# Chunk-selected attention followed by a hard-swish MLP on one core: second batch's keys and queries loaded in two parts, weights asked for earlier, results of batches 1 to 3 turned by DMA

## The chip, the cores and the metric

The kernel runs on 1 core of one Trainium2 chip. The metric is the device time of an execution in microseconds (us), lower is better. The kernel before takes 296.59 us (median of 3 runs, 296.14 to 297.43).

A core has a matrix engine (PE, with its weight loads shown apart as PEld), a vector engine (DVE), a scalar engine (ACT), a general engine (POOL) and a queue engine (SP) that here only issues DMAs. DMAs can be issued from SP, ACT and POOL; each engine works through its own list of instructions in order.

## The reference

Attention of 4 batches, 8 heads, 768 tokens, head size 64. For each query an upper bound of its score with each chunk of 32 keys is made from the chunk's minima and maxima. The 6 chunks with the largest bounds are kept, everything else is masked, and softmax and the product with the values follow. The result, 3072 tokens of 512 channels, goes through an MLP of 512 to 2048 to 512 with a hard-swish between.

```python
k_min = np.min(k_chunks, axis=3); k_max = np.max(k_chunks, axis=3)
ub = np.sum(np.maximum(q[:, :, :, None, :] * k_min[:, :, None, :, :],
                       q[:, :, :, None, :] * k_max[:, :, None, :, :]), axis=-1)
ub = np.where(causal, ub, -1000000000.0)
top_chunks = np.argsort(ub, axis=-1)[..., -top_k:]
...
scores = np.where(mask, scores, -1000000000.0)
scores = scores - np.max(scores, axis=-1, keepdims=True)
attn = np.exp(scores)
attn = attn / (np.sum(attn, axis=-1, keepdims=True) + 1e-09)
...
x = np.ascontiguousarray(attn_out.transpose(0, 2, 1, 3)).reshape(B * S, H * D)
...
h = x @ w_in
relu6 = np.clip(h + 3.0, 0.0, 6.0)
g = h * relu6 / 6.0
return (g @ w_out).astype(np.float32)
```

All inputs and the output are float32.

## The kernel before

The heads are taken two at a time (a pair, 16 pairs, 4 to a batch), the tokens of a batch in two halves of 384. A unit is two pairs of one half, so a batch has four units: units 0 to 3 are batch 0, units 4 to 7 batch 1, and so on. Batch b, half h of the MLP needs the attention results of all four pairs of that half.

For a unit the steps are these. Keys and queries come into SBUF. In batch 0 they come as token blocks (`load_quad`, the DMAs of L144) and PE turns them (L298). From batch 1 on they come as 32-by-32 squares with 128 bytes to a row (`load` and `squares`, the DMAs of L152) and DVE turns them (L308, tiles KF and QF). DVE reduces the keys of each chunk to maximum and minimum (L320, L321, tile KMA) and POOL subtracts. ACT makes relu of the queries (L330, QR). PE makes the bounds (L351, UBT), for all four pairs of a half together from batch 1 on, ACT or DVE copies them out (UBS), PE turns them back (L361, UBN), DVE finds the sixth largest and the selection (L370 to L388, SELA), PE turns that (L394, MP) and ACT and DVE copy it as mask rows into the queries (L179, L181, QLA). PE multiplies keys and queries (L414, SPS), ACT takes the exponential (L424, PT), POOL cuts the diagonal blocks to triangles (L429), PE multiplies with the values (L442, PVP) and DVE divides into the result tile Xb (L450, L451).

For the MLP, `turn_tokens` lets PE turn the 384 tokens by 512 channels of Xb in twelve 128-by-128 transposes (L462, XTP), and `turn_tokens_out` lets DVE copy them from PSUM to SBUF in two copies (L466, tile XT). `hidden` makes 16 groups of four matmuls (L471, HP), ACT makes U from each (L476) and DVE makes GT from U and HP (L481). `result` makes three token blocks of sixteen matmuls (L488, OP), ACT or DVE scales them into OT (L494, L496), and SP stores OT (L500). There are two OT buffers, so the third OT waits until the first is stored. HP, OP, XTP, UBT, UBN, MP and PVP share four PSUM banks.

The order on every engine is made beforehand. `Plan` holds each step with an engine, an assumed length, a rank, what it follows and what buffers it takes and gives. `order` runs through them in assumed time, gives each free engine the ready step of least rank, and the instructions are then written in that order. Nothing is reordered on the chip, so a step that is late holds back all that stands behind it on its engine. A load is a step on SP and an arrival (`arrive`). `load_inputs` puts in the loads of keys and queries of a unit, `load_unit_values` those of the values, and `attend` calls both for the unit three further on, if that unit is of a first half. A load that follows in a buffer waits until the buffer's last reader is done. The DMAs issued from SP and ACT signal through eight semaphores used in turn, so a DMA also waits for the one eight before it.

The weights w_in and w_out come by four DMAs issued from POOL (`load_win`, `load_wout`, L236 and L240), 1024 KB each in SBUF. They are held back: a copy of one element of the values, `seen` (L234), makes them wait until a chosen load of batch 0's values has landed.

Of the kernel before, what the change touches and what calls it, by code (L numbers as in the profile page):

```python
# [13 lines left out]
FP32 = mybir.dt.float32  # L14
# [85 lines left out]
def kernel(  # L100
# [42 lines left out]
            part = (slice(None), slice(None), i) if by_head else (slice(None), i)  # L143
            engine.dma_start(to[part], x[part])  # L144

    def squares(engine, to, x, st):


        for j in range(2):
            for e in range(2):  # L150
                r = 64 * j + 32 * e
                engine.dma_start(to[r:r + 32, :, :],  # L152
                                 x[st["b"], st["h"] + j].rearrange("(c p) d -> p c d", p=CH)[:, :, 32 * e:32 * e + 32])

    def load_quad(n, name, x, engine, by_head=None):

# [3 lines left out]
            st[name, "in", half] = to  # L160
        blocks(engine, to, x, n, by_head)

    def load(st, name, x):

        st[name] = src_pool.tile([P, NCH, 32], FP32, name=name, tag=name.lower())
        squares(nc.sync, st[name], x, st)

    def load_quad_values(n):
        blocks(nc.sync, VS[:, n % 2, units[n][1] * HB:units[n][1] * HB + HB, :, :], v, n, None)
# [60 lines left out]
    def load_win(part):  # L230

        if part == 0:
            seen = const.tile([1, 1], FP32, name="seen")
            nc.gpsimd.tensor_copy(seen[:], VS[0:1, 1, NBLK - 1, 3, 0:1])  # L234
        c0, c1 = part * DFF // 2, (part + 1) * DFF // 2
        nc.gpsimd.dma_start(WIN[:, :, c0:c1], moe_w_in[:, c0:c1].rearrange("(a p) n -> p a n", p=P))  # L236

# [217 lines left out]

    def turn_tokens(g, a):
        if a == 0:
            g["XT"] = GT_pool.tile([P, KT_HID, HS], BF16, name="XT", tag="xt")
        XTP = g["XTP", a] = bank("XTP", [P, 2, HS], BF16)
        for kt in range(a, a + 2):  # L460
            for t in range(HB):
                nc.tensor.transpose(XTP[:, kt - a, t * P:(t + 1) * P],  # L462
                                    X_tiles[g["b"], g["half"]][:, t, kt * P:(kt + 1) * P], IDENTB[:])

    def turn_tokens_out(g, a):
        nc.vector.tensor_copy(g["XT"][:, a:a + 2, :], g["XTP", a][:])  # L466

    def hidden(g, f):
        HP = g["HP", f] = bank("HP", [P, HS])
        for kt in range(KT_HID):  # L470
            nc.tensor.matmul(HP[:], lhsT=WIN[:, kt, f * P:(f + 1) * P], rhs=g["XT"][:, kt, :],  # L471
                             start=(kt == 0), stop=(kt == KT_HID - 1))

    def hidden_relu(g, f):
# [32 lines left out]
    def later(f, *args):  # L507
        return lambda *engine: f(*args, *engine)
# [10 lines left out]
    def load_inputs(n, after=()):  # L519
        two, half = units[n]  # L520
        for name, x in (("KS", k), ("QS", q)):
            if n == 0:
                plan.room[name.lower()] -= 1
                for st in two:
                    there[name, st["pair"], 0] = add("DMA", 0.75, 0)
            elif n < 4:
                arrive((name, two[0]["pair"], half), "SP", 1.6, 1.8, later(load_quad, n, name, x, nc.sync), take=[name.lower()])
                there[name, two[1]["pair"], half] = there[name, two[0]["pair"], half]
        if n >= 4:
            for st in two:  # L530
                for name, x in (("KS", k), ("QS", q)):
                    arrive((name, st["pair"], 0), "SP", 2.2, 2.5, later(load, st, name, x), after=after, take=[name.lower()])
                    there[name, st["pair"], 1] = there[name, st["pair"], 0]

    def load_unit_values(n, after=()):
        two, half = units[n]
# [14 lines left out]
    load_unit_values(3)  # L551
    for name, f, length in (("WIN", load_win, 5.6), ("WOUT", load_wout, 6.2)):
        for part in range(2):
            arrive((name, part), "POOL", 0.9, length, later(f, part), after=[there["V", 2, 1]])


    vs = ["gt", 2 * H // 2]
# [68 lines left out]
    def attend(u):  # L626
# [15 lines left out]
        for i, st in enumerate(two):  # L642
            p = st["pair"]
            need = [mask[i, 0], mask[i, 1]] + made["EB", p % 6] + made["Q", p, half] + made["K", p, half]
            if half == 1:
                need += made["K", p, 0]
            parts = []
            tiles = len(PLAN[half])
            for t in range(tiles):
                cols = max(c0 + w for _, _, w, c0 in PLAN[half][t])  # L650
                a = add("PE", 2 * cols / 2370 + 0.02, r + 8.0 * (i * tiles + t) / (2 * tiles), later(scores, st, half, t),
                        after=need + ([order_of_scores] if order_of_scores else []), take=["s"])
                order_of_scores = a
                begun.append(a)
                free.setdefault(("KL", p), []).append(a)
                free.setdefault(("QL", st["q", half]), []).append(a)
                e = add("ACT", 0.08 + 2 * cols * 0.845e-3, r, later(exponentials, st, half, t), after=[a], take=["pt"],
                        give=[["s", 1]])
                parts.append(e)
                for jb, q0, w, c0 in PLAN[half][t]:  # L660
                    if q0 == jb * P:
                        parts.append(add("POOL", 0.4, r - 15, later(triangle, st, half, t, c0), after=[e]))
            if st["b"] == 0:
                parts.append(add("ACT", 0.45, r - 3, later(cast_values, st, half), after=[there["V", p, half]], give=[vs]))
                parts.append(made["ones", p])
                if half == 1:
                    parts.append(made["V", p])
                else:
                    made["V", p] = parts[-2]
            else:  # L670
                if half == 0:
                    made["V", p] = add("POOL", 0.9, r - 6, later(cast_values, st, half),
                                       after=[there["V", p], made["ones", p % 6]] + free.get(("VB", p - 6), []), give=[["vt", 1]])
                parts.append(made["V", p])
            key = st["b"], half
            a = add("PE", 0.4 if half == 0 else 0.95, r + 1, later(values, st, half), after=parts + finished.get(key, [])[-1:],
                    take=["m"] if finished.get(key) else ["m", "x"],
                    give=[["pt", 1] for _ in range(tiles)])
            if i == 1:
                if 4 <= n + 3 < len(units) and units[n + 3][1] == 0:  # L680
                    load_inputs(n + 3, begun[:1])
                    load_unit_values(n + 3, begun[:1])
            free.setdefault(("VB", p), []).append(a)
            finished.setdefault(key, []).append(
                add("DVE", 0.72, r + 1, later(values_out, st, half), after=[a] + finished.get(key, []),
                    give=[["m", 1]]))
# [9 lines left out]
    for (b, half), xs in finished.items():  # L696
        g = dict(b=b, half=half)
        x = ["x", 2]
        xt, before = [], []
        for a in range(0, KT_HID, 2):  # L700
            m = add("PE", 0.35, r, later(turn_tokens, g, a), after=xs + before, take=["m"] + (["xt"] if a == 0 else []), give=[x])
            before = [m]
            xt.append(add("DVE", 0.5, r - 2000, later(turn_tokens_out, g, a), after=[m], give=[["m", 1]]))
# [47 lines left out]
```

## Time and profile before

| | |
|---|---|
| Time, median of 3 runs | 296.59 us (296.14 to 297.43) |
| Time of the profiled execution | 297.46 us |
| Span of the profiled execution, first to last instruction | 295.7 us |
| PE busy with HP (L471), 512 matmuls | 91.1 us |
| PE busy with OP (L488), 384 matmuls | 90.1 us |
| PE busy with SPS (L414), 320 matmuls | 51.1 us |
| ACT busy with PT (L424), 96 | 85.4 us |
| ACT busy with U (L476), 128 | 71.7 us |
| DVE busy with GT (L481), 128 | 66.8 us |
| PE transposes of Xb (L462), 96 | 38.8 to 249.9 us, first and last start |
| Bytes moved by DMA | 29.81 MB |

The page of the profile gives, for the one core, the busy time of each engine, the span in 40 slices of 7.4 us with the busy share of each slice in tenths, the chain of waits that ended last, followed back from the last instruction, and the costliest groups of instructions by line. The trace behind it can be asked for one line or tile, for the order of instructions of one engine in a window, for the busy time of each engine in a window, and for DMA traffic by queue in a window. Times in it are microseconds from the start of the span. In a row of the chain or of a timeline the first number is the start, the second the time it took, and a mark such as x4 says how many instructions are merged into the row. Engine names with a q (SPq, ACTq) are the engine's issuing of DMAs and its waits, which are not counted as busy time.

### The profile page before, as it was taken

Reading aid. Unit: us, or ns where it says so; the run is one execution under the profiler, and the core shown is the slowest. Engines: PE = TensorE matmul, PEld = TensorE weight load, DVE = VectorE, ACT = ScalarE, POOL = GpSimd, SP = SyncE. Lnnn points to the kernel's source line nnn. Section 1 sums busy time; section 2 is a strip of 40 time slices with the busy share of each in tenths; the row PEclk is TensorE's granted clock in tenths of the full one; section 3 lists DMA queues with packets and bytes.
Section 4 is the critical chain, followed back from the end, with each engine's and each line's share of the span. In section 5 each row is a group of like instructions: output and inputs, shape, how many; then the busy total and the mean of one; then the engine's idle time right before and its main releaser. Section 6 shows DMA issues by size and latency. Waiting matters only on the chain.

```text
span 295.7 us, 6670 instructions
## 1 busy us (share of the span) xinstructions
PE 270.6 (92%) x2384; PEld 161.3 (55%) x2384; DVE 210.7 (71%) x643; ACT 203.1 (69%) x334; POOL 131.5 (44%) x296
## 2 busy tenths in 40 slices
PE   2788799998799999999899989999999999999994
PEld 1445466644444666654565545556566656545641
DVE  6989656793789889998798988987468513831820
ACT  2769889920865899963769986687469863843821
POOL 7778935465370758775722798721111111000000
PEclk9979799999999999999999999999999999999999
DMA  8999999999304299961289991100110001002011
GB/s 169 217 220 137 192 199 217 187 134 198 96 2 87 66 173 173 137 119 73 62 137 183 133 198 41 39 0 2 42 67 0 2 37 73 1 22 88 0 38 71
DMA packets 119746, 29.81 MB, mean 101 GB/s; under 512 B 113568, under 2 KB 115616, under 8 KB 119712
## 3 DMA queue, kind: packets, MB, share of 16 engines
q1 hardware_dynamic: 114976, 24.78, 46.9%
q0 software_dynamic: 3136, 4.19, 8.3%
q10 hardware_dynamic: 1600, 0.39, 0.7%
q8 instruction: 19, 0.31, 0.5%
q14 instruction: 15, 0.12, 0.2%
HBM read 27.26 MB, written 6.29 MB: 113 GB/s over the span
## 4 chain that ended last, share of the span: by engine, by line
PE 57%; DVE 14%; SPq 10%; ACT 7%; DMA 5%; issue 4%; POOL 2%; DVEq 0%; ACTq 0%; POOLq 0%
PE OP L488 21%; PE HP L471 19%; SPq L152 8%; PE SPS L414 7%; PE PVP L442 4%; PE UBT L351 4%; ACT PT L424 2%; DVE GT L481 2%; DMA out_dram<-OT 2%; DVE KMA L320 2%; DVE KMA L321 2%; DVE QLA L181 1%; DMA KS<-in_k_dram 1%; SPq L174 1%; ACT QLA L179 1%
## 5 line engine op out<-in xcount | busy, mean ns | idle before, releaser
L471 PE MATMUL HP<-XT,WIN 128*128 128x384 bf16 x512 | 91.1, 326 | 4.2 <-DVE GT L481 2.0
L424 ACT ACTIVATE PT<-SPS 128x1024 bf16<-128x1024 f32 (+1 forms) x96 | 85.4, 921 | 9.3 <-PE SPS L414 8.3
L488 PE MATMUL OP<-WOUT,GT 128*128 128x512 bf16 x384 | 90.1, 379 | 0.1
L481 DVE SCALAR_TENSOR_TENSOR GT<-U,HP 128x384 bf16<-128x384 bf16 x128 | 66.8, 549 | 23.8 <-ACT U L476 20.4
L476 ACT ACTIVATE U<-HP,THREE 128x384 bf16<-128x384 f32 x128 | 71.7, 589 | 10.6 <-PE HP L471 6.2
L429 POOL TENSOR_SCALAR_AFFINE_SELECT PT<-PT 128x256 bf16<-128x256 bf16 x96 | 38.2, 413 | 75.4 <-ACT PT L424 73.8
L471 PEld LDWEIGHTS <-WIN 128*128 128x128 bf16 x512 | 48.9, 98 | 36.6 <-issue 6.8
L488 PEld LDWEIGHTS <-GT 128*128 128x128 bf16 x384 | 36.6, 98 | 38.1 <-issue 1.2
L414 PE MATMUL SPS<-QLA,KL 128*128 128x384 bf16 (+2 forms) x320 | 51.1, 281 | 2.0 <-ACT PT L424 1.1
L253 POOL TENSOR_SCALAR_AFFINE_SELECT QLA<-QF 64x384 bf16<-64x384 f32 x64 | 33.3, 520 | 20.1 <-PE SPS L414 11.0
L494 ACT ACTIVATE OT<-OP 128x512 f32<-128x512 f32 x22 | 13.1, 596 | 38.7 <-PE OP L488 31.4
L414 PEld LDWEIGHTS <-KL 128*128 128x128 bf16 x320 | 29.0, 98 | 19.5 <-issue 3.9
L253 POOL TENSOR_SCALAR_AFFINE_SELECT KL<-KF 64x384 bf16<-64x384 f32 x64 | 32.5, 509 | 5.9 <-DVE KF L308 2.8
L442 PEld LDWEIGHTS <-PT 128*128 128x128 bf16 x672 | 24.8, 98 | 7.3 <-issue 1.6
L442 PE MATMUL PVP<-VB,PT 128*128 128x65 bf16 x672 | 26.6, 194 | 1.2 <-POOL PT L429 0.6
L330 ACT ACTIVATE QR<-QF 128x384 f32<-128x384 f32 x32 | 16.7, 526 | 11.2 <-DVE QF L308 10.5
L450 DVE RECIPROCAL RINV<-PVP 128x6 f32<-128x6 f32 x32 | 6.0, 186 | 20.9 <-PE PVP L442 20.8
L181 DVE COPY QLA<-MP 32x384 bf16<-32x384 bf16 x42 | 14.8, 353 | 7.5 <-ACT QLA L179 6.0
L320 DVE TENSOR_REDUCE KMA<-KF 128x12 f32<-128x384 f32 x32 | 17.1, 536 | 3.7 <-PE UBT L351 2.3
L451 DVE TENSOR_TENSOR Xb<-PVP,RINV 128x384 bf16<-128x384 f32 x32 | 17.8, 558 | 1.1
L377 DVE MAX8 T<-UB 128x8 f32<-128x24 f32 x192 | 17.7, 167 | 0.0
L321 DVE TENSOR_REDUCE KMA<-KF 128x12 f32<-128x384 f32 x32 | 17.2, 539 | 0.0
(55 smaller groups left out, 203.6 us busy)
## 6 DMA issues: line engine op xcount, KB each, us to landing
out_dram<-OT SPq DMA_DIRECT2D x24, 256.0 KB, 2.0
KS<-in_k_dram SPq DMA_DIRECT2D x52, 96.0 KB, 3.8
QS<-in_q_dram SPq DMA_DIRECT2D x48, 96.0 KB, 3.7
VT<-in_v_dram SPq DMA_DIRECT2D x24, 192.0 KB, 4.1
WIN<-in_moe_w_in_dram POOLq DMA_DIRECT2D x2, 1024.0 KB, 12.0
WOUT<-in_moe_w_out_dram POOLq DMA_DIRECT2D x2, 1024.0 KB, 22.0
VS<-in_v_dram SPq DMA_DIRECT2D x12, 128.0 KB, 3.8
KS<-in_k_dram SPq DMA_DIRECT2D x9, 128.0 KB, 3.8
```

What stands on the lines that cost most here:

```text
L152: engine.dma_start(to[r:r + 32, :, :], x[st["b"], st["h"] + j].rearrange("(c p) d -> p c d", p=CH)[:, :, 32 * e:32 * e + 32])
L253: nc.gpsimd.affine_select(out=to, in_=x, pattern=[[0, n]], compare_op=A.is_ge, fill=0.0, base=0, channel_multiplier=0)
L320: nc.vector.tensor_reduce(out=over, in_=chunks, axis=X_AXIS, op=A.max)
L321: nc.vector.tensor_reduce(out=low, in_=chunks, axis=X_AXIS, op=A.min)
L414: nc.tensor.matmul(SP[:, j, c0:c0 + n], lhsT=KLS[st["pair"] % 6][:, j, jb * P:(jb + 1) * P], rhs=st["QL", half][:, j, at:at + n], start=Tr ...
L424: nc.scalar.activation(PT[:, :, 0:cols], SP[:, :, 0:cols], ACT.Exp, scale=scale)
L429: nc.gpsimd.affine_select(out=PT[:, :, c0:c0 + P], in_=PT[:, :, c0:c0 + P], pattern=[[0, 2], [1, P]], compare_op=A.is_ge, fill=0.0, base=0 ...
L442: nc.tensor.matmul(PVP[:, j, n, :], lhsT=PT[:, j, c0:c0 + P], rhs=st["VB"][:, jb, j, :], start=(jb == 0), stop=(jb == qb))
L471: nc.tensor.matmul(HP[:], lhsT=WIN[:, kt, f * P:(f + 1) * P], rhs=g["XT"][:, kt, :], start=(kt == 0), stop=(kt == KT_HID - 1))
L476: nc.scalar.activation(U[:], g["HP", f][:], ACT.Relu, bias=THREE[:], scale=1.0)
L481: nc.vector.scalar_tensor_tensor(out=g["GT"][:, f, :], in0=g["U", f][:], scalar=6.0, in1=g["HP", f][:], op0=A.min, op1=A.mult)
L488: nc.tensor.matmul(g["OP", t][:], lhsT=g["GT"][:, f, t * P:(t + 1) * P], rhs=WOUT[:, f, :], start=(f == 0), stop=(f == FT - 1))
```

## The change

1. Batch 1's keys and queries (units 4 to 7) are loaded in two parts: `squares` moves either the first or the second 12 of the 24 chunks, so each of the 32 DMAs of 32x24x32 elements becomes two of 32x12x32. Both parts go to the same tile, which is taken with the first. `load_inputs` is called for units 4 to 7 each, and the values of batch 1 are loaded between first and second parts. Batches 2 and 3 are loaded in one part as before.
2. The weights wait for the values of quad 0's second half instead of quad 1's second half, the load that stands one place earlier on SP.
3. For batches 1 to 3 one DMA issued from ACT transposes Xb into XT, SBUF to SBUF, 128 by 1536 elements of bf16. PE's twelve transposes and DVE's two copies stay for batch 0 alone. XT is laid out by token block first, and `hidden` reads it so.

```diff
-    def squares(engine, to, x, st):
+    def squares(engine, to, x, st, half):
+        at = slice(0, NCH) if half is None else slice(half * HC, (half + 1) * HC)
         for j in range(2):
             for e in range(2):
                 r = 64 * j + 32 * e
-                engine.dma_start(to[r:r + 32, :, :],
-                                 x[st["b"], st["h"] + j].rearrange("(c p) d -> p c d", p=CH)[:, :, 32 * e:32 * e + 32])
+                engine.dma_start(to[r:r + 32, at, :],
+                                 x[st["b"], st["h"] + j].rearrange("(c p) d -> p c d", p=CH)[:, at, 32 * e:32 * e + 32])
...
-    def load(st, name, x):
-        st[name] = src_pool.tile([P, NCH, 32], FP32, name=name, tag=name.lower())
-        squares(nc.sync, st[name], x, st)
+    def load(st, name, x, half=None):
+        if not half:
+            st[name] = src_pool.tile([P, NCH, 32], FP32, name=name, tag=name.lower())
+        squares(nc.sync, st[name], x, st, half)
...
-            nc.gpsimd.tensor_copy(seen[:], VS[0:1, 1, NBLK - 1, 3, 0:1])
+            nc.gpsimd.tensor_copy(seen[:], VS[0:1, 0, NBLK - 1, 3, 0:1])
...
-            g["XT"] = GT_pool.tile([P, KT_HID, HS], BF16, name="XT", tag="xt")
+            g["XT"] = GT_pool.tile([P, HB, KT_HID, P], BF16, name="XT", tag="xt")
...
-        nc.vector.tensor_copy(g["XT"][:, a:a + 2, :], g["XTP", a][:])
+        nc.vector.tensor_copy(g["XT"][:, :, a:a + 2, :].rearrange("p t k r -> p k t r"),
+                              g["XTP", a][:].rearrange("p k (t r) -> p k t r", t=HB))
+
+    def turn_tokens_by_dma(g):
+        g["XT"] = GT_pool.tile([P, HB, KT_HID, P], BF16, name="XT", tag="xt")
+        nc.scalar.dma_start(g["XT"][:].rearrange("p t k r -> p (t k) r"), X_tiles[g["b"], g["half"]][:].rearrange("p t c -> p (t c)"),
+                            transpose=True)
...
-            nc.tensor.matmul(HP[:], lhsT=WIN[:, kt, f * P:(f + 1) * P], rhs=g["XT"][:, kt, :],
+            nc.tensor.matmul(HP[:], lhsT=WIN[:, kt, f * P:(f + 1) * P], rhs=g["XT"][:, :, kt, :],
...
-                    arrive((name, st["pair"], 0), "SP", 2.2, 2.5, later(load, st, name, x), after=after, take=[name.lower()])
-                    there[name, st["pair"], 1] = there[name, st["pair"], 0]
+                    if n < 8:
+                        arrive((name, st["pair"], half), "SP", 2.2, 1.3, later(load, st, name, x, half), after=after,
+                               take=[name.lower()] if half == 0 else [])
+                    elif half == 0:
+                        arrive((name, st["pair"], 0), "SP", 2.2, 2.5, later(load, st, name, x), after=after, take=[name.lower()])
+                        there[name, st["pair"], 1] = there[name, st["pair"], 0]
...
-            arrive((name, part), "POOL", 0.9, length, later(f, part), after=[there["V", 2, 1]])
+            arrive((name, part), "POOL", 0.9, length, later(f, part), after=[there["V", 0, 1]])
...
                     load_inputs(n + 3, begun[:1])
-                    load_unit_values(n + 3, begun[:1])
+                    if n + 3 != 4:
+                        for m in {5: (4, 5)}.get(n + 3, (n + 3,)):
+                            load_unit_values(m, begun[:1])
+                    if n + 3 == 5:
+                        load_inputs(6, begun[:1])
+                        load_inputs(7, begun[:1])
...
-        for a in range(0, KT_HID, 2):
+        if b > 0:
+            m = add("ACT", 0.6, r - 2000, later(turn_tokens_by_dma, g), after=xs, take=["xt"])
+            xt.append(add("DMA", 2.0, -500, after=[m], give=[["x", 1]]))
+        for a in range(0, KT_HID if b == 0 else 0, 2):
```

Because `Plan` sorts all steps anew, the order of instructions on every engine differs from the first load of batch 1 on. In the changed kernel's order SP issues, after batch 0's loads: 32 first parts of batch 1, 6 value loads, 24 second parts, the first store of OT, the last 8 second parts among two more stores and two value loads, then batch 2. Before, it issued 32 whole loads and 6 value loads ahead of the first store.

## The prediction

> **What bounds the kernel now.** I read the busy times, then the slices and the chain of waits, then PE in windows of 5 us, then the queues.
>
> ```profile
> PE 270.6 (92%) x2384; PEld 161.3 (55%) x2384; DVE 210.7 (71%) x643; ACT 203.1 (69%) x334; POOL 131.5 (44%) x296
> ...
> PE   2788799998799999999899989999999999999994
> ...
> DMA  8999999999304299961289991100110001002011
> ...
> PE 57%; DVE 14%; SPq 10%; ACT 7%; DMA 5%; issue 4%; POOL 2%; DVEq 0%; ACTq 0%; POOLq 0%
> ```
>
> PE is the bound: 270.6 of 295.7 us, and of its 25.1 us of idle time the windows put some 12 in the first 35 us and 3.1 at the very end. So the time falls only by work taken off PE or by closing the other 10 us. Two places hold most of those, and the chain names them.
>
> ```profile
> 69.51 0.62 SPq L174
> 70.24 4.08 DMA out_dram<-OT
> 74.42 0.60 ACT OT L494
> ...
> 170.68 3.71 DMA QS<-in_q_dram
> 174.58 0.58 DVE QF L308
> 177.02 1.56 PE UBT L351 x32
> ...
> 188.41 0.67 PE XTP L462 x12
> ...
> 248.75 1.39 PE XTP L462 x24
> 250.14 10.65 PE HP L471 x64
> ```
>
> At 70 us the first store of OT goes out only when SP has got through the loads of batch 1. ACT's third OT waits for that buffer until 74.42, and everything behind it on ACT waits too. At 145 to 171 us the chain is SP issuing batch 3's loads, and PE stands 1.4 us before its bounds at 177.02. The last rows are the transposes that the change removes.
>
> ```profile
> 28.36 13.48 SPq L152 DMA_DIRECT2D KS<-in_k_dram  x4
> 41.94 12.38 SPq L152 DMA_DIRECT2D QS<-in_q_dram  x4
> ...
> 70.24 0.58 SPq L500 DMA_DIRECT2D out_dram<-OT  x1
> ...
> 133.99 11.26 SPq L500 DMA_DIRECT2D out_dram<-OT  x3
> 145.30 2.23 SPq L152 DMA_DIRECT2D KS<-in_k_dram  x4
> ```
>
> That is SP in order of time. While the weights come, four loads take 13 us instead of 2.2. The DMA view says why: from 30 to 50 us the weights' queue (q0) holds the engines and the loads (q1) move 2490 packets, 125 to the us. From 57 to 70 us they move 14057, 1080 to the us.
>
> ```profile
> q0 software_dynamic: 2670, 3.73, 106.9%
> q1 hardware_dynamic: 2490, 0.31, 19.9%
> ```
>
> **The change part by part.**
>
> *Transposes off PE.* Batches 1 to 3 have six turns of twelve. Four take 0.67 us each (188.41), the last two 1.39 together: 4 x 0.67 + 1.39 = 4.1 us, all of it on a PE that is busy before and after. Gain 4.1. DVE loses 12 copies of 546 ns (the line of L466), 6.6 us. PE waited for DVE's GT 2.0 us in all, mostly where DVE is full (23.95 of 25 us from 105 to 130). I take 0.5 us of that as gained, bounds 0 and 1.5.
>
> *The DMAs that replace them.* The trace has no DMA transpose. What it holds of ACT is bounded from below by a plain DMA of 128 rows issued there, 2.12 us for four (L144), 0.53 each, and from above by the same 393,216 bytes cut into 128-byte pieces, 3072 pieces or four L152 loads at 0.55, 2.2 us. Since it is one instruction I take 0.53. Where it stands on ACT is read in the changed order. Three of the six stand among OT and UBS while PE runs OP, or in the last 47 us, where ACT is busy 22.2 us: hidden by that slack. One (batch 1, half 1) stands between two exponentials with four OP to each: hidden too, and 1 us if it takes 2.2. Two (batch 2) stand among U and exponentials, where ACT has nothing over (155 to 160: 4.95 of 5): 2 x 0.53 = 1.1 us lost. Landing lies between 2.0 us (median of the stores) and 6 us (four loads issued in 2.2 and landing 3.8 after). Between issue and first HP, PE has 24 OP, UBN and PVP for batch 1 half 0, about 5.5 us, 10 us for half 1 and over 20 us for the rest. So landing costs nothing, or 0.5 us at the upper bound.
>
> [...]
>
> *Weights sooner.* POOL makes its copy with three casts fewer ahead of it (0.5 to 0.6 each), so the weights start and end 1.7 us earlier, at 52.7 instead of 54.4 (the second request at 30.0 lands 24.4 later). The first HP at 41.82 had no wait on a DMA, so nothing is won there. POOL's casts behind the four issues (3.5 us) come later, for the mask rows of a pair scored near 38 us: hidden, 1 us if not.
>
> *Two parts.* The number of packets is the same, the number of requests is not: 32 more for SP. By 28 us eight half loads are out (four held to 26 us as before, then 0.55 each). Until 52.7, at 125 packets to the us, 3090 packets or eight halves land, so with eight in flight some 21 of the first 62 requests are issued then. All first parts are in by about 59 us instead of whole loads by 73. The bounds of batch 1 move up from 86.7 us to behind 36 OP (36 x 0.216 = 7.8 us) and one PVP, about 67 us, and their data and DVE's 8 us of turning and reducing are ready by then: no wait. But the first store of OT is now request 63 instead of 39. The 41 left take 0.50 each (2.01 us for SP's first four, with idle engines; a half needs only 384/1080 = 0.36 of engine time): 52.7 + 20.5 = 73.2, landed 2.0 later at 75.2. ACT's third OT (0.60) and two mask rows (0.48 each) stand in line for that, and the scores of batch 1 wait for the mask rows: 76.8. PE has run out of OP, UBN, MP and the first HP at 72.5. Idle 4.3 us, in place of 2.7 from 70 to 80 before: lost 1.6. After it ACT has 16 U (0.5), 8 exponentials (1.5 a pair) and 4 QR (0.5), 16 us against 13.7 of PE; the last U lie under OP, and I leave it as even with the 1.3 us of idle time of 80 to 108 before. Bounds: 3 us gained (store issued at 70 as before) to 8 lost (below).
>
> *Batch 3's loads* stand behind two stores on SP instead of three, and only its second quad behind the third, so they are asked for one OT sooner. I take the 1.4 us wait at 177 as gone. Bounds 0 and 2.5.
>
> Sum: -4.1 - 0.5 + 1.1 + 1.6 - 1.4 = -3.3. The profiled execution took 297.46, 1.8 more than its span, and would take 294.2. It lies 0.9 above the median, so the median is forecast at 296.6 - 3.3 = 293.3 us.
>
> **Rivals.**
>
> *The queue gives it all back (slower).* One mechanism: a half load costs SP as much as a whole one did. From 54.37 to 70.24 us, 22 requests took 0.72 each. At that price the store goes at 52.7 + 29.5 = 82.2, lands with its 4.08 at 86.3, and the mask rows are there at 87.9: PE idle 15.4 instead of 2.7, so 293.3 - 1.6 + 12.7 = 304.4. The kernel is no faster than before once the idle time is 7.6 us, which is a price of 0.58 for each request. For it: requests of 768 packets run at 0.55 to 0.62 from 92 to 107 us. Against it: those keep the DMA engines full, halves don't. About half of this effect gives 299.
>
> *The transpose is dear on ACT.* At 2.2 us each, 1.67 more at the two U places, 1 among exponentials, 0.5 for landing and 0.4 in the tail: 293.3 + 5.2 = 298.5. [...]
>
> *PE's gain is taken up elsewhere.* PE's 4.1 us become idle time, since in batches 1 and 2 ACT and DVE are full beside it (105 to 130: 23.6 and 23.95 of 25) and only the tail's 1.39 us and the 1.4 at 177 are kept, less 1.6 and 1.1: 296.5, no change. Against it: DVE gets relief in the same stretches, and from 188 to 249 PE is busy 60.3 of 60.5.
>
> *The early first parts bring more.* If the store goes out at 70, 3 us instead of -1.6: 288.7.
>
> **How the numbers follow.** About 0.5% (1.5 us) can be told from no change. The forecast has 0.41 (290 to 295), the early store 0.13, no change 0.19, the queue 0.15, dear transposes 0.12. Faster is the first two and a little of the dear case at its cheap end, 0.55; same 0.19; slower the rest, 0.26. Leaving out half of the early store's lower tail and the ends of the two slower cases, 8 in 10 lie from 288 to 300.5.
>
> **What would show it.** No XTP of batches 1 to 3 on PE, and PE's busy time down by 4. In ACT's order the transposes' issue, 0.5 or 2 us. On SP the first store at 73 (right), 70 (gain) or over 76 (queue), and the third OT 2 to 4 us after it. Bounds of batch 1 near 67 us. No chain through SP from 145 to 171. I am wrong if PE stops before HP for XT, if SP's half loads are issued at over 0.58 us, or if the gaps of PE between 60 and 110 us sum to more than 10.

## The result, and the profile after

The changed kernel takes 301.47 us (median of 4 runs, 300.71 to 303.19) where the kernel before took 297.01 (4 runs, 296.14 to 299.65): a ratio of 1.0138, with a 95% interval from 1.0095 to 1.0181. It is slower by 4.5 us (4.1 by the ratio); 293.3 had been forecast. The profiled execution took 301.35 us, its span is 299.6.

The page of the changed kernel, busy times, slices and the chain of waits by engine:

```profile
PE 268.5 (90%) x2312; PEld 157.1 (52%) x2312; DVE 202.5 (68%) x630; ACT 200.5 (67%) x335; POOL 130.6 (44%) x296
...
PE   2877899995499999998999797999999999999994
...
PE 51%; DVE 20%; SPq 9%; ACT 7%; DMA 7%; issue 4%; POOL 1%; ACTq 0%; DVEq 0%; POOLq 0%
```

PE has the 72 transposes less and is busy 268.5 us in place of 270.6, so 31.1 us of the span are idle in place of 25.1. The busy time falls by 2.1, the idle time grows by 6.0. The tenth and eleventh slices, 67 to 82 us, have dropped to 5 and 4 tenths. The windows of PE show the two kernels from 60 to 110 us (length, then busy time and instructions of PE, PEld, DVE, ACT and POOL, the granted clock of PE, the DMA share and GB/s), before and after:

```profile
60.00:110.00 50.00, 46.07 (x387) 25.72 (x386) 40.70 (x138) 29.84 (x51) 27.03 (x58) 1.00 0.61 104
```

```profile
60.00:110.00 50.00, 41.99 (x317) 22.40 (x316) 36.38 (x127) 23.75 (x43) 27.17 (x58) 0.90 0.78 139
```

PE is idle 8.0 us here instead of 3.9, and for a part of the time it is not at full speed: the granted clock averages 0.90 over the window. From 110 to 200 us, where batches 2 and 3 are prepared, it is idle 7.0 us (90 less 83.02 busy) instead of 4.8. Up to 60 us it is better, 11.6 against 12.6. The longest gap between 110 and 200 us, and DVE's wait in front of it, where GT stands behind the turning of a load of batch 3's keys:

```profile
171.29 0.58 DVE L310 STREAM_TRANSPOSE KF<-KS 128x384 f32<-128x384 f32 x1 [2.00 <-DMA KS<-in_k_dram]
```

```profile
172.36 1.08 PE L444 MATMUL PVP<-VB,PT 128*128 128x65 bf16 x30 [1.59 <-DVE GT L489]
```

The chain of waits of the changed kernel and its list of waits (time waited, how often, longest) name the place:

```profile
74.66 0.47 SPq L153
...
75.23 2.18 DMA out_dram<-OT
77.51 0.61 ACT OT L502
```

```profile
POOL VB L185 <- DMA VT<-in_v_dram: 19.5, 3, 16.6
ACT OT L502 <- DMA out_dram<-OT: 10.4, 1, 10.4
...
PE SPS L416 <- ACT QLA L181: 7.4, 2, 6.7
```

The chain runs through one half load of SP after the other, 0.47 us of each and a gap, until the first store of OT is issued at 75.23. It lands 2.18 us later, ACT's third OT follows at 77.51, then the mask rows, and PE, which had stood for 6.7 us, starts the scores at 78.65. POOL waited even longer for the values of batch 1's last pair (VT), which SP asks for after the store, at 80.36; the kernel before asked for them at 70.91. SP in order of time, in the changed kernel and then in the kernel before:

```profile
57.32 5.08 SPq L176 DMA_DIRECT2D VT<-in_v_dram  x6
...
75.23 0.41 SPq L508 DMA_DIRECT2D out_dram<-OT  x1
...
80.36 1.00 SPq L176 DMA_DIRECT2D VT<-in_v_dram  x2
```

```profile
70.91 1.39 SPq L174 DMA_DIRECT2D VT<-in_v_dram  x2
```

What PE does behind its wait, in its timeline:

```profile
78.65 1.61 PE L416 MATMUL SPS<-QLA,KL 128*128 128x384 bf16 x6 [6.71 <-ACT QLA L181]
80.06 2.77 PE L479 MATMUL HP<-XT,WIN 128*128 128x384 bf16 x8
...
86.98 1.46 PE L479 MATMUL HP<-XT,WIN 128*128 128x384 bf16 x8
```

Eight HP take 2.77 us here; a little later eight take 1.46.

### The profile page after: what moved, and what is told of

It is laid out like the page before. It is cut to its first block, busy times and chain, and to the rows that moved or that the text cites. A ratio compares the mean times of both kernels' runs of the same rounds, so it can differ in the third digit from the quotient of the medians.

```text
span 299.6 us, 6592 instructions
## 1 busy us (share of the span) xinstructions
PE 268.5 (90%) x2312; PEld 157.1 (52%) x2312; DVE 202.5 (68%) x630; ACT 200.5 (67%) x335; POOL 130.6 (44%) x296
## 4 chain that ended last, share of the span: by engine, by line
PE 51%; DVE 20%; SPq 9%; ACT 7%; DMA 7%; issue 4%; POOL 1%; ACTq 0%; DVEq 0%; POOLq 0%
PE OP L496 18%; PE HP L479 17%; SPq L153 7%; PE SPS L416 7%; DVE GT L489 5%; DMA KS<-in_k_dram 4%; PE PVP L444 4%; PE UBT L353 4%; ACT PT L426 2%; DVE QLA L183 2%; DVE T L379 2%; DVE KMA L323 2%; DMA QS<-in_q_dram 2%; DVE KMA L322 2%; ACT QLA L181 2%
## 5 line engine op out<-in xcount | busy, mean ns | idle before, releaser
L479 PE MATMUL HP<-XT,WIN 128*128 128x384 bf16 x512 | 94.7, 330 | 1.8 <-DVE GT L489 1.5
L426 ACT ACTIVATE PT<-SPS 128x1024 bf16<-128x1024 f32 (+1 forms) x96 | 86.7, 930 | 11.5 <-PE SPS L416 8.1
L416 PE MATMUL SPS<-QLA,KL 128*128 128x384 bf16 (+2 forms) x320 | 52.0, 282 | 9.4 <-ACT QLA L181 7.4
L502 ACT ACTIVATE OT<-OP 128x512 f32<-128x512 f32 x24 | 14.3, 595 | 41.3 <-PE OP L496 28.8
L322 DVE TENSOR_REDUCE KMA<-KF 128x12 f32<-128x384 f32 x32 | 17.1, 533 | 3.6 <-PE UBT L353 2.2
L185 POOL TENSOR_SCALAR_AFFINE_SELECT VB<-VT 128x768 bf16<-128x768 f32 x12 | 10.7, 903 | 19.8 <-DMA VT<-in_v_dram 19.5
```

Source lines behind the costliest of these rows:

```text
L322: nc.vector.tensor_reduce(out=over, in_=chunks, axis=X_AXIS, op=A.max)
L416: nc.tensor.matmul(SP[:, j, c0:c0 + n], lhsT=KLS[st["pair"] % 6][:, j, jb * P:(jb + 1) * P], rhs=st["QL", half][:, j, at:at + n], start=Tr ...
L426: nc.scalar.activation(PT[:, :, 0:cols], SP[:, :, 0:cols], ACT.Exp, scale=scale)
```

## The experiments

A median is given with that of the kernel before on the same chip and the ratio of the two with its interval. Runs that did not share a chip are compared by their medians; the kernel before took 297.0 to 298.4 us beside them, so such a difference is good to about 1 us.

### One part of the change at a time

Three kernels, each the kernel before with one of the three parts of the change as its diff shows it: the DMA transposes (turn_only), the loads in two parts (parts_only), the copy `seen` (weights_only).

> The kernel before with the DMA transposes alone. Theory A (the loss is the wait of the third OT for the first store, which the half loads push back): this kernel has whole loads, so it keeps most of PE's 4.1 us and pays two to three holds of ACT of 1.44 us: 294 to 296, faster than before. Theory B (the transposes lose the time, by 1.44 us of ACT each and 3.7 us to landing): 299 or more, PE waiting for XT or ACT full at six places.

Measured: 297.48 against 297.46, ratio 1.0003 (0.9971 to 1.0035). In the profiled execution PE is busy 267.5 us of a span of 297.1, and all of what it saves has become idle time. Neither expectation was met.

> The kernel before with batch 1's keys and queries in two parts alone. SP has 66 requests ahead of the first store, four more than the changed kernel's 62. Theory A: the store goes about 2 us later than the changed kernel's 75.23, PE stands 8 to 9 us instead of 6.7 and the matrix engine's clock falls after it: 303 to 307. Theory B: no slower than before, 295 to 297.5.

Measured: 302.56 against 297.46, 1.0176 (1.0146 to 1.0206). The first store goes out at 78.35, PE waits 8.0 us for the mask rows. This is a little below the range of theory A and far above that of B: the loss is in this part.

> The kernel before with the weights asked for earlier alone. Both theories: within 1.5 us of before. If the 2.4 us by which the changed kernel began its first OP matmuls sooner (56.29 against 58.70 us) come from this part, OP begins near 57 us here; if they come from the new order or the clock, it begins near 59.

Measured: 299.16 against 297.46, 1.0038 (0.9998 to 1.0079), no clear change. The first OP starts at 57.6 in place of 59.6, but the first store is issued at 70.62 as before, and PE waits 2.6 us for ACT's third OT as before: what the start wins is lost there.

### Does the wait for the store alone make the loss?

after_ot3 gives the changed kernel a third OT buffer, in the same order of instructions (UBS and UB get two buffers in place of three to make room).

```diff
-    o_pool = ctx.enter_context(tc.tile_pool(name="op", bufs=2))
+    o_pool = ctx.enter_context(tc.tile_pool(name="op", bufs=3))
...
-        u["UBS"] = work.tile([P, HS], FP32, name="UBS", tag="ubs")
+        u["UBS"] = work.tile([P, HS], FP32, name="UBS", tag="ubs", bufs=2)
...
-        UB = u["UB"] = work.tile([P, HB, 4, NCH], FP32, name="UB", tag="ub")
+        UB = u["UB"] = work.tile([P, HB, 4, NCH], FP32, name="UB", tag="ub", bufs=2)
```

> The changed kernel with three OT buffers in place of two (UBS and UB get two in place of three to make room), the order of every engine unchanged. Theory A: the third OT no longer waits for the first store, PE's 6.7 us wait falls under 1.5 us, the clock stays up: 301.5 - 5.2 - 2.5 = about 294. Theory B, or a loss that lies in the new order of batches 1 to 3 (theory C): 299 to 301.5.

Measured: 304.94 against 297.46, 1.0246 (1.0199 to 1.0292), slower still, and outside both expectations. The waits of this kernel:

```profile
POOL VB L185 <- DMA VT<-in_v_dram: 23.0, 4, 18.2
PE PVP L444 <- POOL PT L431: 14.1, 6, 11.2
```

The third OT waits no more, and the scores start at 71.7. Now PE stands 11.2 us before PVP: POOL's triangles stand behind the cast of the last pair's values, and SP asks for those values only at 83.46, after the second parts and two stores. (The first store goes out at 78.33 here, with the same requests ahead of it as in the changed kernel: its time differs by some 3 us between profiled executions, and what makes it differ is not shown.) Behind the wait that was taken away stood a longer one with the same origin. The theory had to be widened: everything that SP issues after the second parts is late.

### The second parts behind the stores

late_seconds is the changed kernel, with the loads of the second parts put in later.

```diff
-                    if n + 3 == 5:
-                        load_inputs(6, begun[:1])
-                        load_inputs(7, begun[:1])
+                if n == 4:
+                    load_inputs(6, begun[:1])
+                    load_inputs(7, begun[:1])
```

> The changed kernel, with one thing moved: the second parts of batch 1's keys and queries (32 requests) are asked for once batch 1's first scores are on their way, so that on SP they stand behind the first three stores and behind the last pair's values; the first store is request 39 again. Theory A (SP's backlog of 32 more requests made the store, and with it ACT, PE and the clock, late): the first store is issued at about 61 to 63 us, ACT's third OT waits under 2 us, PE has no gap over 2 us between 60 and 90, its clock there stays 1.00, and the time is 292 to 296. Theory B (the parts cost elsewhere, by a packet's price or by ACT's hold of 1.44 us for each DMA transpose): the gap goes, and the time stays above 299. Under either, the second parts could now be late themselves: then DVE waits for a DMA of KS or QS between 85 and 110 us.

Measured: 293.61 against 298.35, 0.9836 (0.9790 to 0.9882). SP in order of time, and PE from 60 to 110 us:

```profile
63.55 1.82 SPq L508 DMA_DIRECT2D out_dram<-OT  x2
65.94 1.04 SPq L176 DMA_DIRECT2D VT<-in_v_dram  x2
```

```profile
60.00:110.00 50.00, 46.96 (x362) 25.75 (x364) 41.56 (x139) 30.22 (x54) 25.93 (x57) 1.00 0.73 140
```

The first two stores are issued from 63.55 on, the last pair's values at 65.94 in place of 80.36. PE is idle 3.0 us in place of 8.0, at full clock. The same transfers, the same 32 further requests, 7.9 us less (9.0 by the ratios): theory A holds, and the loss lies in the place of the second parts on SP.

### What a request costs

tiny_requests is the kernel before with 32 requests that carry next to nothing.

```diff
+        if st["b"] == 1:
+            for j in range(4):
+                at = 4 * (2 * (st["pair"] - H // 2) + (name == "QS")) + j
+                nc.sync.dma_start(TINY[:, at, :], x[st["b"], st["h"], 32 * j:32 * j + 32, 0:3])
...
+    TINY = const.tile([32, 32, 3], FP32, name="TINY")
```

> The kernel before, with 32 more requests on SP: behind each of the eight loads of batch 1's keys and queries four loads of 32 rows of 12 bytes, which nobody reads. They bring 1024 packets of 12 bytes and none of the other parts of the change. Theory A (a request has a price of its own on SP, about 0.5 us, whatever it carries): SP has 38 requests to issue after the weights in place of 22, the first store goes out at 74 to 78 us instead of 70.2, and the time is 300 to 304. Theory B (the price follows the packets, 384/1080 = 0.36 us for a half load and 0.03 for one of these): the store goes out at 70 to 71.5 and the time is 297 to 298.5.

Measured: 309.37 against 297.03, 1.0412 (1.0378 to 1.0446), beyond both. SP, after the weights are in:

```profile
67.64 2.07 SPq L152 DMA_DIRECT2D QS<-in_q_dram  x4
69.76 1.93 SPq L170 DMA_DIRECT2D TINY<-in_q_dram  x4
...
81.09 0.49 SPq L505 DMA_DIRECT2D out_dram<-OT  x1
```

Four whole loads, of 768 rows each, take 2.07 us of SP, four requests of 32 rows 1.93: 0.52 and 0.48 each, and a half load of 384 rows took 0.50. So from 67.64 us on, with the weights in, a request of these sizes cost SP about half a microsecond, 12 bytes to a row or 128, and the 32 further ones ahead of the store delayed it by 10.9 us (70.24 to 81.09). PE waits 11.3 us there.

### What does standing still cost beyond itself?

after_warm is the changed kernel with PE repeating one hidden tile during the wait, eleven times, after_warm14 fourteen times.

```diff
-        for kt in range(KT_HID):
-            nc.tensor.matmul(HP[:], lhsT=WIN[:, kt, f * P:(f + 1) * P], rhs=g["XT"][:, :, kt, :],
-                             start=(kt == 0), stop=(kt == KT_HID - 1))
+        for _ in range(11 if (g["b"], g["half"], f) == (0, 1, 0) else 1):
+            for kt in range(KT_HID):
+                nc.tensor.matmul(HP[:], lhsT=WIN[:, kt, f * P:(f + 1) * P], rhs=g["XT"][:, :, kt, :],
+                                 start=(kt == 0), stop=(kt == KT_HID - 1))
```

> The changed kernel, with the first hidden tile of batch 0's second half computed eleven times over into the same bank, so that PE multiplies for some 7 us more where it otherwise stands for the mask rows. The wait itself stays. If the half-rate matmuls behind the wait come from PE's standing still: the eight HP after it take about 1.46 us instead of 2.77, the granted clock stays 1.00, and the time falls by 2 to 3 us to 298.5 to 299.5. If the clock falls for another cause (the time since the start, the power of other engines): the HP still take about 2.7 us and the time is 301.5 or a little more.

> The changed kernel with the first hidden tile of batch 0's second half computed fourteen times over: with eleven PE still stood for 1.65 us and the clock fell to 0.50 for 3 us behind it. If standing still is what lowers the clock, no matter when: PE has no idle time over 0.7 us between 70 and 84, the granted clock stays 1.00 there, the eight HP behind the wait take 1.46 us and the time is 1 to 2.5 us below that with eleven (303.4). If the clock falls anyway: the HP take 2.7 us and the time is no lower than 303.

Measured: 303.36 against 298.35, 1.0175 (1.0115 to 1.0234), and 305.14 against 297.03, 1.0261 (1.0209 to 1.0314). Neither was faster. With eleven, two windows of PE:

```profile
80.00:81.00 1.00, 0.68 (x5) 0.39 (x5) 0.35 (x1) 0.56 (x2) 0.00 (x0) 1.00 0.94 297
81.00:82.00 1.00, 1.00 (x7) 0.56 (x5) 1.00 (x12) 0.97 (x3) 0.00 (x0) 0.54 0.66 107
```

PE was busy to 78.5 and stood only 1.65 us, and still the clock fell to half at 81.1, so the eight HP again took 2.77 us. With fourteen there was no such gap, the clock stayed at 1.00 and the eight HP took 1.46; but PE then waited at PVP for POOL's triangles until 88.54, and the clock fell there instead. In both, SP issued the store later than in the changed kernel, at 76.53 and 77.03 in place of 75.23, and the last pair's values at 81.67 and 82.18 in place of 80.36. So with fourteen repeats the clock was at 1.00 up to 89 us, and in the changed kernel at 0.50 from 74 to 84; what the half clock costs by itself these runs don't show, since behind it PE runs into the late values anyway.

### Where PE's 4.1 us went

Two pairs of kernels differ in the transposes and in nothing else. before_ot3 is the kernel before with the third OT buffer, turn_ot3 the same with DMA transposes. late_no_turn is late_seconds with the transposes of batches 1 to 3 on PE, where DVE copies them out again.

> The kernel before with three buffers for OT, the control for the run with transposes. If the wait of ACT's third OT for the first store is what costs PE its 2.7 us between 70 and 80: 293.5 to 295. If the next wait takes its place (POOL's triangles behind the cast of a value load, as with the halves): 296 to 299.

> The kernel before, with the DMA transposes and with three buffers for OT (UBS and UB get two in place of three, to make room). The transposes alone changed nothing (ratio 1.0003). Theory A (their 4.1 us of PE fell into the same waits of ACT and DVE that bound the stretches of batches 1 and 2): removing the wait for the first store gives what it gives without transposes and no more, so this and the same kernel without transposes differ by under 1.5 us. Theory B (the wait for the first store swallowed the gain): the two differ by 3 to 4 us, and this one takes 290 to 292.

> The run in which the second parts come behind the first stores (293.6 us), with batches 1 to 3 transposed on PE again as before the change. Theory A (the transposes' 4.1 us of PE fall into waits of DVE and ACT): the time is within 1.5 us of the other, 292.5 to 295. Theory B (they count once SP holds nothing up): 296.5 to 298.

Measured: before_ot3 294.91 and turn_ot3 294.22 against 298.35, ratios 0.9889 (0.9839 to 0.9938) and 0.9873 (0.9813 to 0.9934). late_no_turn 294.13 against 297.03, 0.9887 (0.9859 to 0.9915), beside 293.61 and 0.9836 with DMA transposes. The third buffer alone brings 3 us, so the wait for the first store did cost the kernel before that much. But with or without that wait the exchange of the transposes brings 0 to 0.7 us (at most 1.5 by the ratios). That fitted the rival in which DVE and ACT take up whatever PE gains. The other theory was tried next: that issuing the transposes from ACT gives the gain back. late_none leaves the turning out: the hidden layer of batches 1 to 3 multiplies the tokens turned for batch 0, and neither PE, DVE, ACT nor a DMA spends time on turning their own. late_sp issues the six DMA transposes from SP.

```diff
-        nc.scalar.dma_start(g["XT"][:].rearrange("p t k r -> p (t k) r"), ...
+        nc.sync.dma_start(g["XT"][:].rearrange("p t k r -> p (t k) r"), ...
...
-            m = add("ACT", 0.6, r - 2000, later(turn_tokens_by_dma, g), after=xs, take=["xt"])
+            m = add("SP", 1.44, r - 2000, later(turn_tokens_by_dma, g), after=xs, take=["xt"])
```

> The run in which the second parts come behind the first stores (293.6 us), with the turning of batches 1 to 3 left out altogether: neither PE nor a DMA transposes their results, and their hidden layer multiplies the tokens of batch 0 in their place. PE has the 4.1 us less, and ACT holds no DMA transpose (6 x 1.44 us). Theory A (DVE, ACT and POOL bound the stretches of batches 1 and 2, so that PE's time is not wanted there): 292 to 294, PE idle some 26 us. Theory B (the DMA transposes' hold of ACT eats what PE gains): 289 to 291.

> The run in which the second parts come behind the first stores (293.6 us), with the six DMA transposes issued by SP in place of ACT. Theory A (the hold of 1.44 us on ACT is of no account): 293 to 294.5, or longer where a transpose waits on SP behind loads and PE waits for XT. Theory B (ACT's hold eats the gain): 290 to 292, with ACT's waits shorter by some 8 us.

Measured against 297.34: late_none 286.67, 0.9641 (0.9610 to 0.9671); late_sp 290.30, 0.9760 (0.9722 to 0.9797). Theory B holds, and late_none lies even below its range. Without any turning the time is 6.9 us lower than with DMA transposes issued by ACT (5.8 by the ratios), so these transposes do cost; with SP as the issuer 3.3 of them are had (2.3 by the ratios). What the other 3.6 us hang on, the landing, SP's time or the order, no run tells apart. late_sp is also 3.8 us below late_no_turn: work taken off PE and DVE is worth time there after all. No run divides this between PE's 4.1 us of transposes and DVE's 6.6 us of copies, which go together. PE from 100 to 260 us, transposes issued by ACT and then by SP:

```profile
100.00:260.00 160.00, 151.77 (x1378) 90.65 (x1390) 114.73 (x366) 118.37 (x190) 63.23 (x143) 1.00 0.49 92
```

```profile
100.00:260.00 160.00, 155.60 (x1410) 93.20 (x1409) 114.59 (x367) 119.95 (x194) 63.45 (x143) 1.00 0.51 93
```

The idle time of PE halves, from 8.2 to 4.4 us. How one hold gets into the path is seen in late_seconds at 150 us, in ACT's timeline and then in PE's:

```profile
149.77 0.58 ACT L484 ACTIVATE U<-HP,THREE 128x384 bf16<-128x384 f32 x1 [0.49 <-PE HP L479]
150.60 1.34 ACTq L473 DMA_TRANSPOSE XT<-Xb  x1
152.05 1.52 ACT L484 ACTIVATE U<-HP,THREE 128x384 bf16<-128x384 f32 x3 [1.70 <-DVE UB L372]
```

```profile
149.93 2.17 PE L479 MATMUL HP<-XT,WIN 128*128 128x384 bf16 x12
151.97 0.34 PE L396 MATMUL MP<-IDENTB,SELA 128*128 128x128 bf16 x3
153.27 1.46 PE L479 MATMUL HP<-XT,WIN 128*128 128x384 bf16 x8 [0.96 <-DVE GT L489]
```

ACT makes a U, has nothing to do until DVE is through with Xb at 150.57, and then issues the transpose until 151.94. PE has meanwhile filled three banks with HP, from 149.93 on. Their U start only at 152.05, GT follows, and PE stands 0.96 us until a bank is free. Behind three of the six holds PE has a gap in the trace (0.49 us at 140.31, 0.96 here, 0.31 at 249.51); the rest of the gain has no single place. (The row of 152.05 puts ACT's idle time down to DVE's UB, an event of that moment; the transpose stands in it.) The runs show what the issuer is worth, not that the 1.44 us alone are its price: the wait for Xb and the order on both queues change with it.

### The sooner weights

late_no_weights is late_seconds with the weights asked for where the kernel before does. turn_weights_ot3 is the changed kernel with whole loads and the third OT buffer.

```diff
-            nc.gpsimd.tensor_copy(seen[:], VS[0:1, 0, NBLK - 1, 3, 0:1])
+            nc.gpsimd.tensor_copy(seen[:], VS[0:1, 1, NBLK - 1, 3, 0:1])
...
-            arrive((name, part), "POOL", 0.9, length, later(f, part), after=[there["V", 0, 1]])
+            arrive((name, part), "POOL", 0.9, length, later(f, part), after=[there["V", 2, 1]])
```

> The run in which the second parts come behind the first stores (293.6 us), with the weights asked for where the kernel before asks for them. The first OP started at 56.0 to 56.8 us in the profiles that had half loads and sooner weights, at 57.6 with sooner weights alone, at 59.0 to 59.6 without them. Theory A (the sooner weights bring the start forward, against what I had reckoned): the first OP starts at 58.5 to 59.5 and the time is 295.5 to 297. Theory B (the start depends on chance alone): it starts at 56 to 57 and the time is 293 to 294.5.

> The changed kernel with whole loads, and three buffers for OT: transposes by DMA and sooner weights, without parts, and without the wait for the first store. If the parts bring something of their own once SP does not hold the store up, it is slower than the run with late second parts (293.6): 294.5 to 296. If they bring nothing: 292.5 to 294.

Measured against 297.34: late_no_weights 296.63, 0.9978 (0.9952 to 1.0004); turn_weights_ot3 292.65, 0.9837 (0.9815 to 0.9859). The result tiles of late_no_weights and of late_seconds, up to 64 us (shortest, median and longest in ns, then first and last start):

```profile
L496 PE MATMUL OP<-WOUT,GT x21: 376/379/379, 59.5 to 63.9; 128*128 128x512 bf16 x21
```

```profile
L496 PE MATMUL OP<-WOUT,GT x30: 377/379/379, 56.4 to 64.0; 128*128 128x512 bf16 x30
```

The sooner weights bring the start forward by 3.1 us and the end by 3.0 (4.2 by the ratios) in this kernel. A second pair that differs in the weights alone, turn_ot3 and turn_weights_ot3 with whole loads and the third OT buffer, gives less: 294.22 and 292.65, 1.6 us (1.1 by the ratios, whose intervals overlap). So the sooner weights are worth 1 to 4 us where the first store doesn't swallow it. The first HP has no wait on a DMA in either, but it stands elsewhere in the written order: it starts at 38.2 us in place of 41.9, and fills gaps of the attention of batch 0. Whole loads do as well as late second parts.

### All that helped together

late_ot3, late_sp_ot3 and whole_sp_ot3 put the third OT buffer into late_seconds, into late_sp, and, with SP issuing, into the kernel with whole loads. Their diffs are those above.

> The run in which the second parts come behind the first stores (293.6 us), with three buffers for OT. Its third OT has hardly a wait on a store left, so if nothing else is late the time is the same, 292.5 to 294.5; a gain of over 1 us would mean that stores still hold ACT up further on, a loss of over 1 us that the third buffer brings another order that suits worse.

> All that helped, with the parts: second parts behind the first stores, sooner weights, DMA transposes issued by SP, three buffers for OT. The run without the third buffer took 290.3 us, and the third buffer brought 0.1 us before. Expected 289.5 to 291. If over 292, the third buffer's order costs what it brings.

> All that helped, without the parts: whole loads, sooner weights, DMA transposes issued by SP, three buffers for OT. With ACT issuing the transposes this took 292.65 us. If ACT's hold is what the transposes cost wherever they stand, SP brings some 3 us here too: 288.5 to 290. If the gain of 3.3 us came from the order that went with late parts: 292 to 293.

Measured: late_ot3 293.47 against 297.03, 0.9885 (0.9833 to 0.9937); late_sp_ot3 289.78 and whole_sp_ot3 290.80 against 298.29, 0.9718 (0.9685 to 0.9751) and 0.9744 (0.9716 to 0.9772). With whole loads too, SP in place of ACT brings 1.9 us (290.80 beside 292.65; 2.8 by the ratios, whose intervals lie apart): between the two expectations, nearer to the first. The two best kernels beat the kernel before by 2.8% and 2.6%, and their intervals overlap: loading in two parts brings nothing that these runs can tell. What brings the time down is the sooner weights, the store out of the way and the transposes off both PE and ACT.

## Why the prediction was wrong, point by point

A way from the kernel before to the changed one leads over two of the runs: 297.0 to 294.1 (late_no_turn: sooner weights, parts, no wait for the store), to 293.6 (DMA transposes from ACT), to 301.5 (second parts ahead of the stores): -2.9, -0.5 and +7.9 (-3.4, -1.5 and +9.0 by the ratios). The forecast of 293.3 is almost the time of the kernel without the backlog, but that is another kernel than the one forecast, and the nearness is luck: three terms other than the store's were wrong too, in both directions. None of the three signs of being wrong that the text had named came: only 0.2 us of a weight load waited for XT, SP's half loads took 0.50, and PE's gaps from 60 to 110 us sum to 8.0. They watched the issue price and the gaps, not the values behind the store nor the clock.

- **The first store, +1.6.** This is the step that failed. The mechanism was the right one, a half load cost SP about as much as a whole one (0.50 us, beside 0.52 in tiny_requests), and 0.50 us was the right price. But the text put the store at 73.2 and PE's gap at 4.3 us; it was 75.23 and 6.7, mostly because the six value loads in the line took 5.08 us, 0.85 each instead of 0.50. And what follows was "left as even": the last pair's values, asked for 9.4 us later than before (80.36 against 70.91) and worth an 11.2 us wait of PE once the store's wait is away (after_ot3), and the half clock, 10.2 us long, were in no term. Alone the parts cost 5.1 us (parts_only, 5.2 by the ratio); in the full change their place on SP costs 7.9 (late_seconds), about the 8 that the text had as the worst bound of this term. The runs do not divide the 7.9 us among the store, the values and the clock. The early first parts did what was forecast, the bounds of batch 1 ran at 65.1 us (67 forecast), but kernels with whole loads take as little time (turn_weights_ot3 beside late_ot3), so no gain from it can be told at the end. The rival "the queue gives it all back" names this mechanism, with 304.4 by a price of 0.72 for each request; at 0.50 it gives the loss as well, through what stands behind the store.
- **Transposes off PE, -4.1 and -0.5.** The size was near: late_sp, which pays on SP and not on ACT, is 3.8 us below late_no_turn. In the change ACT took it back.
- **The DMA transpose on ACT, +1.1.** Mis-sized. The hold is 1.44 us (median of six), not 0.53, and within the bounds of 0.53 and 2.2. With SP as the issuer the time falls by 2 to 3 us, with late second parts as with whole loads, so at least that much of 6 x 1.44 = 8.6 us reached the end. A part of it comes in the last batch (0.31 us), which had been called hidden by ACT's slack: ACT has slack in that stretch, but the hold stands between two U that PE waits for. Landing took 3.7 us at the median, within its bounds, and only 0.2 us of a weight load waited for XT: as forecast. The rival with 2.2 us for each (298.5) has more than was measured: the holds on ACT were 1.29 to 1.52 us in the changed kernel.
- **Sooner weights, 0.** Worth 3.0 us in one pair of kernels and 1.6 in another, where the store doesn't swallow it. The weights landed at 53.1 us, 1.3 sooner and not 1.7. "The first HP had no wait on a DMA" was true and not enough: the written order, not a wait, kept the first HP behind.
- **Batch 3's loads, -1.4.** Did not come. The wait before the bounds shrank from 1.39 to 0.80 us, but DVE now waited 2.00 us for a load of batch 3's keys and PE 1.59 us for the GT behind it, and the chain still runs through SP's loads, from 165 to 176 us. PE's idle time from 110 to 200 us grew by 2.2 us, from 4.8 to 7.0. It is 6.9 with the transposes alone (turn_only), 5.0 with the parts alone (parts_only), and falls from 6.9 (late_seconds) to 3.7 once SP issues the transposes (late_sp): the growth comes with the transposes, and mostly with their issue on ACT.
- **The rival "PE's gain is taken up elsewhere"** gave no change for the transposes alone, and turn_only measured that. Its reason, that DVE and ACT are full beside PE, is refuted as far as ACT's own work goes: in late_sp the gain is had beside the same work. What took it up was the issue on ACT.

## What to carry to other kernels

Splitting a load is not free when one queue issues everything: count the requests that stand ahead of a store or a late load, price them at the queue's issue time (0.50 us for a half load here), and follow every later request of that queue, not only the first one that waits. A DMA that replaces work on the busiest engine has an issuer, and the issuer is held (1.44 us at the median on ACT here): put it on the queue that has time, here SP, which brought 2 to 3 us, and look at what the bound engine waits for behind each hold (gaps of 0.31, 0.49 and 0.96 us behind three of six in late_seconds). An experiment that takes away one wait and makes the kernel slower has not refuted the cause if the next wait hangs on the same queue.

## What the runs showed of the hardware

- With the weights in, a DMA request held SP for 0.48 us with 32 rows of 12 bytes (tiny_requests, four in 1.93 us at 69.76), 0.50 with 384 rows of 128 bytes (changed kernel, four in 2.00 us at 69.03) and 0.52 with 768 such rows (tiny_requests, four in 2.07 us at 67.64). While the weights came, four loads of 768 rows took 13.48 us (kernel before). In the changed kernel, value loads of 768 rows of 256 bytes took 0.50 each as a pair (1.00 us at 80.36) and 0.85 each as six in a row (5.08 us at 57.32).
- A DMA transpose of 128 x 1536 two-byte elements within SBUF, twelve 128 x 128 blocks, held its issuer for 1.29 to 1.52 us on ACT (changed kernel) and for 1.28 to 2.62 us on SP, longest between loads (late_sp). It landed after 3.7 us at the median in the changed kernel and 3.8 in late_sp (from 3.6 in late_sp to 6.2 in turn_only).
- PE's granted clock went to 0.50 for 3.4 us (after_warm, turn_only), 10.2 (the changed kernel) and 13.7 (after_ot3), read to a hundredth from windows of 1 us: about one, three and four times 3.4. It fell behind a gap of 1.65 us (after_warm), one of 2.69 (turn_only) and two of 0.98 and 0.94 (after_warm14); behind gaps adding to 2.66 us between 70 and 80 us in the kernel before it did not. What length is enough these runs don't show.
